# A batch-2 decode block on one core: the last V block moved ahead of half of wo, the attention tail made uniform, and the gated MLP computed as rows

## The chip, the cores and the metric

The kernel runs on one core of one Trainium2 chip. The metric is device time in microseconds (us) of one execution, median of several. "Span" is the time from the first to the last instruction in the one profiled execution; it is about 2 us shorter than the timed figure. TensorE, VectorE and ScalarE are PE, DVE and ACT in the profile's lines, the DMA-issuing engine is SP.

## The reference, cut to what matters

```python
# x: (2, 1, 512) bf16; K and V caches: (2, 32, 8192, 128) bf16; wq: (512, 4096); wo: (4096, 512)
# W_gate, W_up: (512, 1376); W_down: (1376, 512)
q = layernorm(x) @ wq                        # 32 heads of 128
p = softmax(q . K^T * 128**-0.5)             # one query per head, 8192 keys
h = x + (p . V) @ wo
y = layernorm(h)
out = h + (relu(y @ W_gate) * (y @ W_up)) @ W_down
```

K and V are 268 MB; all weights together are 12.6 MB. The heads are worked off in 16 "quads" of four heads (eight per batch row). One quad's K is 8 MB (8 x 2^20 bytes, and so wherever this text says MB of a load), its V another 8 MB.

## The kernel before

VectorE multiplies each K tile by the replicated query and adds along the head dimension; ScalarE exponentiates; TensorE multiplies the weights into V. K tiles rotate through two buffers, V through one. The main loop (cut):

```python
    for n in range(N - 1):                    # N = 16 quads
        scores(n, HALVES if n == 0 else (0, T))
        if n + 2 < N:
            load_k(n + 2)                     # waits until scores(n) has read its buffer
        collect()                             # VectorE: pick the lanes out of a finished V product
        ...                                   # gather, normalise, at chosen n
        weighted_v(n)
        if n + 2 < N:
            load_v(n + 1)                     # waits until weighted_v(n) has read the one V tile
```

After the loop everything that follows attention goes into the K buffer that quad 14 leaves, and the DMA queue gets, in this order: all of wo, the last V in four pieces, gate, up, W_down.

```python
    W = kring.tile([P, RING], bf16, tag="k", name="W")
    ...                                       # wo of quads 0-3, 4-5, 6 in rows of 16, 8, 4 KB
    nc.sync.dma_start(out=wol, in_=A_wo[LQ * G * Dh:, :].rearrange("(h d) n -> d h n", d=P))  # 1 KB rows
    CUTS = (0, T // 2, T * 7 // 8, T * 15 // 16, T)
    load_v(N - 1, CUTS)
    ...                                       # gate, up, W_down
    scores(N - 1)
    ...
    for k in range(NK):                       # 28 wo matmuls: 7 of 8 quads of both batch rows
        g = k % (P // Q) * Q
        nc.tensor.matmul(out=ar_ps[g:g + B], lhsT=oc[:, k, :], rhs=wo_sb[:, k, :], ...)
    ar = opool.tile([P, D], f32, tag="row")
    nc.scalar.activation(out=ar, in_=ar_ps, func=ACT.Copy)
    o15 = ps_o.tile([P, TG * Dh], f32, tag="o")
    v_moving(N - 1, o15, 0, CUTS[1], last=False)          # V15, first half
    for c in range(KC):                                   # rows to columns, f32
        nc.tensor.matmul(out=a_ps[:, c, :], lhsT=columns(ar)[:, c, :], rhs=row_of[:, 0:B], ...)
    ...
    v_moving(N - 1, o15, CUTS[1], CUTS[2], first=False)   # V15, up to 7/8
    o_sum = lanes_of(o15)
    ...                                                   # the last eighth with V stationary
    for h in range(G):                                    # the last quad alone: 16 small matmuls
        project(wol[:, h, :], ol[:, h, :], last=(h == G - 1))
```

So only the last quad's share, 16 bf16 matmuls with wo stationary, stands between V15 and the second layernorm. The MLP keeps its weights stationary: 44 matmuls of 128x128 by 2 columns each for gate and for up, and the results lie as columns, 11 blocks by 2, ready for W_down.

The softmax here doesn't subtract the row's maximum and nothing guards it: scores larger than these inputs give would overflow.

## Time and profile before

| | before |
|---|---|
| time, median | 661.2 us |
| span of the profiled execution | 659.4 us |
| DMA, 281 MB | busy in every part of the span but the end |
| VectorE busy | 609.6 us (92%) |
| TensorE busy | 119.5 us (18%) |

The first lines are from the page of the kernel before: the span, then busy tenths in 40 slices for VectorE and DMA.

```profile
span 659.4 us, 3234 instructions
...
DVE  2899999999999999999999999999999998999952
...
DMA  9999999999999999999999999999999999999996
```

DMA is full from beginning to end. To see how the stream runs I added up the bytes of the trace's DMA packets in order of their end: 8 MB land every 19.35 us, one load behind the other. By this count the bytes up to the end of each of the last loads have landed at these times (us from the span's start): K15 594.98, V14 613.9, all of wo 624.1, V15 643.2, gate 646.7, up 650.0, W_down 655.2. Neighbouring loads overlap, so a load's own last packet can come later than its count (gate 648.15, up 651.50). 8,388,608 bytes in 19.35 us are 433.5 GB/s. The Trainium skill ("DMA: Bandwidth & Descriptors", Where 436 GB/s comes from) gives 435.2 GB/s as the ceiling of the ports into SBUF; the trace agrees to within half a per cent, so rearranging work can gain at most half a per cent in the middle of the kernel.

What is left is the end. The chain of waits of the kernel before, from 560 us on (start, duration, what):

```profile
554.14 41.31 DMA k<-in_A_k_cache_dram
...
595.47 17.24 DVE k L222
...
629.57 2.29 DVE sc L231
...
636.38 3.16 PE ar_ps L452 x28
...
642.02 1.96 PE a_ps L459 x8
...
645.75 0.36 DVE osb L266
...
648.37 0.67 PE a_ps L434 x16
...
650.34 1.71 PE gate_ps L510 x44
...
654.38 1.17 PE y_ps L466 x31
...
655.55 0.52 PE y_ps L466 x12
```

K15 is released at 554.14 and lands 41 us later: the queue is that far ahead, and what VectorE does between two quads is hidden by it. From 595.47 VectorE works 36.4 us on quad 15; from 631.86 a chain of short TensorE and VectorE links follows. It ends at 656.38, just after the stream does at 655.2: compute and DMA end together.

### The profile page before, as it was taken

How to read it: one execution, taken by the hardware profiler on the slowest of the kernel's cores; microseconds unless marked ns; L12 is line 12 of the kernel's file. 1: busy time of each engine (PE TensorE's matmuls, PEld its weight loads, DVE VectorE, ACT ScalarE, POOL GpSimd, SP SyncE). 2: the span in 40 equal slices, each digit the busy share in tenths (PEclk: the TensorE clock that was granted, in tenths of full speed). 3: DMA queues.
4: the chain of work that ended last, by engine and by line, in shares of the span. 5: the costliest groups of instructions: out<-in, count | busy, mean ns of one | idle time of the engine just before them, and what ended most of it. 6: DMA issues, size and time to landing. Idle time of an engine off the chain costs nothing.

```text
span 659.4 us, 3234 instructions
## 1 busy us (share of the span) xinstructions
PE 119.5 (18%) x1341; PEld 58.6 (9%) x1341; DVE 609.6 (92%) x225; ACT 55.8 (8%) x142; POOL 2.5 (0%) x8
## 2 busy tenths in 40 slices
PE   2100302003030210303012130301202030020446
PEld 1000101001010100101001110100001010010225
DVE  2899999999999999999999999999999998999952
ACT  2201001010101001010101001010010101001020
POOL 1000000000000000000000000000000000000000
PEclk9555755757565575756557575555757555575656
DMA  9999999999999999999999999999999999999996
GB/s 382 445 445 445 395 433 446 437 445 418 417 445 437 441 442 398 445 445 426 441 417 433 445 422 441 437 417 441 426 441 441 421 438 426 433 441 433 393 420 259
DMA packets 7314, 281.26 MB, mean 427 GB/s; under 512 B 802, under 2 KB 1412, under 8 KB 2308
## 3 DMA queue, kind: packets, MB, share of 16 engines
q1 hardware_dynamic: 7272, 281.06, 98.9%
q8 instruction: 10, 0.16, 0.1%
q14 instruction: 4, 0.03, 0.0%
q10 hardware_dynamic: 28, 0.01, 0.0%
HBM read 281.06 MB, written 0.00 MB: 426 GB/s over the span
## 4 chain that ended last, share of the span: by engine, by line
DVE 62%; DMA 33%; PE 3%; issue 1%; ACT 0%; DVEq 0%
DMA k<-in_A_k_cache_dram 31%; DVE k L222 29%; DVE k L228 28%; DVE sc L231 4%; DMA wq_sb<-in_A_wq_dram 2%; DVE osb L268 1%; DVE qrep L188 1%; PE qps L175 1%; PE o L257 1%; PE ar_ps L452 0%; ACT qrep L186 0%; PE y_ps L466 0%; PE a_ps L459 0%; PE gate_ps L510 0%; PE up_ps L510 0%
## 5 line engine op out<-in xcount | busy, mean ns | idle before, releaser
L222 DVE TENSOR_TENSOR k<-k,qrep 128x32768 bf16<-128x32768 bf16 (+1 forms) x17 | 275.7, 16217 | 8.9 <-DMA k<-in_A_k_cache_dram 8.8
L228 DVE TENSOR_TENSOR k<-k 128x16384 bf16<-128x16384 bf16 (+3 forms) x68 | 266.8, 3923 | 2.3
L257 PE MATMUL o<-v,pm 128*32 128x512 bf16 x1016 | 88.1, 522 | 395.8 <-DMA v<-in_A_v_cache_dram 395.8
L234 ACT ACTIVATE pm<-sc 32x256 bf16<-32x256 f32 x64 | 47.2, 738 | 563.9 <-DVE sc L231 527.6
L257 PEld LDWEIGHTS <-pm 128*32 128x32 bf16 x1016 | 37.9, 127 | 444.8 <-issue 282.3
L231 DVE TENSOR_REDUCE sc<-k 128x256 f32<-128x2048 bf16 (+1 forms) x17 | 36.7, 2161 | 1.6
L307 PE MATMUL rep<-osb,spread 128*64 128x128 f32 (+1 forms) x16 | 5.9, 474 | 110.5 <-DVE osb L268 110.5
L234 ACT ACTIVATION_READ_ACCUMULATOR pm<-sc 32x1 f32 x64 | 15.0, 234 | 0.0
L307 PEld LDWEIGHTS rep<-osb,spread 128*64 128x64 f32 (+1 forms) x16 | 3.2, 257 | 114.1 <-DVE osb L268 114.1
L188 DVE CAST qrep<-qps 32x512 bf16<-32x512 f32 x8 | 5.5, 692 | 7.2 <-ACT qrep L186 7.1
L266 DVE TENSOR_SCALAR osb<-o,turn_of 128x128 f32<-128x128 f32 x10 | 3.4, 344 | 9.2 <-PE o L257 9.2
L268 DVE SCALAR_TENSOR_TENSOR osb<-o,turn_of,osb 128x128 f32<-128x128 f32 x30 | 10.5, 351 | 1.1
L175 PE MATMUL qps<-wq_sb,xnb 128*64 128x512 bf16 x32 | 6.5, 562 | 7.0 <-DMA wq_sb<-in_A_wq_dram 4.8
L186 ACT ACTIVATE qrep<-qps 32x512 bf16<-32x512 f32 x8 | 4.7, 586 | 8.5 <-PE qps L175 5.2
L152 DVE COPY xc<-x_ps 128x8 f32<-128x8 f32 x1 | 0.2, 167 | 4.9 <-PE x_ps L149 4.9
L510 PEld LDWEIGHTS <-W 128*128 128x128 bf16 (+1 forms) x88 | 3.8, 126 | 0.3 <-issue 0.3
L175 PEld LDWEIGHTS <-xnb 128*64 128x64 bf16 x32 | 2.7, 147 | 10.0 <-issue 5.3
L452 PE MATMUL ar_ps<-W,oc 128*2 128x512 bf16 x28 | 3.2, 626 | 1.8 <-DVE oc L357 1.8
L297 PE MATMUL o_l<-lane_of,osb 128*128 128x4 f32 x2 | 0.6, 364 | 12.8 <-DVE osb L268 12.8
L317 DVE TENSOR_TENSOR rep<-rep,pick 128x128 f32<-128x128 f32 x6 | 1.8, 295 | 1.0 <-PE rep L307 0.9
L330 PE MATMUL zb<-zm,same 128*128 128x4 f32 (+2 forms) x12 | 2.3, 306 | 0.3 <-DVE ol_f L298 0.3
L330 PEld LDWEIGHTS zb<-zm,same 128*128 128x128 f32 x12 | 2.1, 258 | 0.8 <-issue 0.4
(92 smaller groups left out, 44.3 us busy)
## 6 DMA issues: line engine op xcount, KB each, us to landing
k<-in_A_k_cache_dram SPq DMA_DIRECT2D x2, 4096.0 KB
wq_sb<-in_A_wq_dram SPq DMA_DIRECT2D x1, 4096.0 KB, 12.3
v<-in_A_v_cache_dram SPq DMA_DIRECT2D x1, 4096.0 KB, 13.3
v<-in_A_v_cache_dram SPq DMA_DIRECT2D x1, 3072.0 KB, 20.2
W<-in_A_wo_dram SPq DMA_DIRECT2D x1, 2048.0 KB
W<-in_B_W_gate_dram SPq DMA_DIRECT2D x1, 1376.0 KB
W<-in_B_W_up_dram SPq DMA_DIRECT2D x1, 1032.0 KB, 27.4
W<-in_A_wo_dram SPq DMA_DIRECT2D x1, 1024.0 KB, 29.0
```

The source lines that it names most:

```text
L175: nc.tensor.matmul(out=qps[h * B * Q:(h + 1) * B * Q], lhsT=xnb[:, c].rearrange("p b q -> p (b q)"), rhs=wq_v[:, c, g:g + QP, h0 + h, :], ...
L186: nc.scalar.activation(out=dst, in_=src, func=ACT.Copy)
L188: nc.vector.tensor_copy(dst, src)
L222: nc.vector.tensor_tensor(out=kp, in0=kp, in1=_view(qrep[:, b, i, :], 0, [[0, hi - lo], [1, Dh]]), op=ALU.mult)
L228: nc.vector.tensor_tensor(out=kp[:, :, 0:half], in0=kp[:, :, 0:half], in1=kp[:, :, half:width], op=ALU.add)
L231: nc.vector.tensor_reduce(out=sc[:, lo:hi], in_=kp[:, :, 0:8], axis=AXIS.X, op=ALU.add)
L234: nc.scalar.activation(out=p_of[ps, :, :, h], in_=sc[ps, :].rearrange("p (g t) -> p g t", t=TG), func=ACT.Exp, accum_out=(zm[ps, b, i:i + ...
L257: nc.tensor.matmul(out=o[g:g + W2], lhsT=_view(pm, (0 if lane else R) + t // TG * W2, [[1, W2]]), rhs=vt[:, t:t + TG, :].rearrange("p t d ...
L268: nc.vector.scalar_tensor_tensor(out=osb, in0=o[:, t * Dh:(t + 1) * Dh], scalar=turn_of[:, t:t + 1], in1=osb, op0=ALU.mult, op1=ALU.add)
L307: nc.tensor.matmul(out=reps[where][at:at + m, max(k - 1, 0), :], lhsT=spread[n_of].rearrange("k u h m -> k (u h m)"), rhs=osb, start=True, ...
L330: nc.tensor.matmul(out=zb, lhsT=lhsT, rhs=z, start=True, stop=True)
L510: nc.tensor.matmul(out=ps[0:w, fc, :], lhsT=lhsT, rhs=hd[:, c, :], start=(c == 0 and fc == 0), stop=(c == KC - 1), skip_group_check=True)
```

## The change

Its intent: treat all eight quads of a row alike, so that one piece of code serves them (gathers of four quads, no special last quad, fewer masks); have V15 earlier, by loading it into V14's tile half by half ahead of the second half of wo; and compute gate and up as rows, 512 columns at a time in three column tiles of TensorE, then transpose the activations back with four matmuls. The diff, cut to its core ("..." marks cuts):

```diff
-    SIZES = (4, 2, 1)
-    FIRST = (0, 4, 6)
+    NS = 4
...
+    load_wo(0)
+    L = N - 1
+    vts[L] = vts[L - 1]
+    weighted_v(L - 1, 0, T // 2)
+    load_part(vts[L], A_v_cache, L, 0, T // 2)
+    weighted_v(L - 1, T // 2, T)
+    CUTS = (T // 2, T * 7 // 8, T)
+    for lo, hi in zip(CUTS[:-1], CUTS[1:]):
+        load_part(vts[L], A_v_cache, L, lo, hi)
+    for k in range(1, NGR):
+        load_wo(k)
+    scores(L)
+    X = kring.tile([P, RING], bf16, tag="k", name="X")      # gate, up, W_down: K15's buffer
...
+    attention_rows(0, NK - JG)                               # first 16 of 32 wo matmuls
+    for lo, hi in zip(CUTS[:-1], CUTS[1:]):
+        weighted_v(L, lo, hi)
     collect()
+    gather()
+    normalize(B - 1, NGR - 1)
+    attention_rows(NK - JG, NK)                              # the other 16
     ar = opool.tile([P, D], f32, tag="row")
     nc.scalar.activation(out=ar, in_=ar_ps, func=ACT.Copy)
...
-    for h in range(G):
-        project(wol[:, h, :], ol[:, h, :], last=(h == G - 1))
+    for c in range(KC):
+        nc.tensor.matmul(out=h_ps[:, c, :], lhsT=ar.rearrange("p (m c) -> p c m", c=KC)[:, c, :],
+                         rhs=row_of[:, 0:B], start=(c == 0), stop=True, skip_group_check=True)
...
+            for j in range(FT):
+                nc.tensor.matmul(out=ps[j * Q:(j + 1) * Q, :],
+                                 lhsT=hd[:, c].rearrange("p a b -> p (a b)"),
+                                 rhs=wgu[:, g, c, offs[j]:offs[j] + MT], ...)
...
+    for r in range(RD):
+        nc.tensor.matmul(out=act_ps[:, r].rearrange("p j b -> p (j b)"),
+                         lhsT=act[0:RW].rearrange("k (m r) -> k r m", r=RD)[:, r, :], rhs=ident..., ...)
```

## The prediction

> **What bounds it now.** The page gives DMA at 9 tenths in 39 of 40 slices and 281 MB, so the stream sets the pace. Adding up the trace's packets in order, 8 MB land every 19.35 us, without a gap, from the first load on: K15 at 594.98, V14 at 613.9, wo at 624.1, V15 at 643.2, gate 646.7, up 650.0, W_down 655.1. The queue is some 40 us ahead (K15 issued at 554.1, landed at 595), so VectorE's small work between quads is hidden. The chain ends: DMA k to 595.45, VectorE scores(15) 36.4 us to 631.86, then 24.5 us of short TensorE and VectorE links to 656.38, output, span 659.4 (661.2 timed). There compute and DMA finish together: the last y_ps matmul waits for the last W_down rows.
>
> **What moves.**
> 1. Masks, collects (10 to 8), gathers, normalising in the loop: some 3 us less VectorE. Off the path: K15's landing does not move. Worth 0.
> 2. V15's first half waits for half of V14's matmuls (start 614.97, 99 ns each: 618.2), while wo's first half is through at 618.3. With the issue, a DMA gap of 1 to 2 us (estimate). Given back: wo's last quad had 1 KB rows and took 2.15 us for 0.5 MB against 1.2 for 0.5 MB of others. W_down still ends near 655.
> 3. Gate, up and W_down now go into K15's tile, so after 631.86; the queue holds V15 and wo until about 644. Gate about 647.5, up 651: before their use.
> 4. Tail. Before, 28 of 32 wo matmuls and their row-to-column products ran before V15's last part; now half of wo, the whole gather and the columns come after it. From the trace's durations (estimate): Exp ends 634.99; z sums and 32 V matmuls to 638.8; x row and 16 wo matmuls (113 ns each) to 640.9; 32 V matmuls to 642.8; four lane steps 1.5, spread 0.8, gather 0.6, normalise 0.2: 646; 16 wo matmuls 1.8; ScalarE copy 0.6; columns 2.0 (the trace: 8 in 2.03); copy, sum, mean 1.0; hd 0.25: 651.7.
> 5. MLP in: 12 matmuls of 512 columns, three side by side. Four side by side take 427 ns a round at clock 0.5, so four rounds 1.7 us for gate, 1.7 for up, against 1.71 and 1.59 before. No gain. The elementwise steps are 512 wide instead of 22: about 0.65 instead of 0.25 each (the 32x512 cast took 0.69), gate's hidden under up. New: four transposing matmuls and a copy, 0.8. Down 48 matmuls, 1.6. End near 658.5, plus 3 us of output.
>
> So some 2 us slower, unless the clock helps. The Trainium skill ("TensorE: Matmul & The Clock Gate", Part 1) says the clock is released by activity in free-running windows of 3413 ns. This trace agrees: 0.91 to 1.00 from 640 to 647, 0.50 before and after 649. Cold for wo and MLP is what I assume; warm would save about 2.5 us.
>
> **Predicted: 663.2 us, 80% range 660.9 to 665.0.** Faster by over 2%: 0.005; within 2%: 0.985; slower by over 2%: 0.01.
>
> **What would show it.** scores(15) ends within 0.5 us of 631.9; DMA shows a dip at 618 to 620 and ends near 655; last lane steps start near 642.9 (before: 645.75); gate_ps starts near 652 (before: 650.34) and takes about 1.7; y_row near 658.5, waiting for compute, not DMA.
>
> **What would make it wrong.** The gap at 618 longer than 3 us, so that wo's second half or gate becomes the wait; three column tiles not running side by side (gate 5 us); fp32 column products cheaper than 2 us; a warm clock through the MLP, giving equality or a small gain.

## The result

The changed kernel takes 663.33 us (median of 6, 662.55 to 663.95) against 661.25 us (median of 6, 661.01 to 661.45): 2.1 us or 0.3% slower. The ratio is 1.0032, with a 95% interval of 1.0019 to 1.0044. Ratios in this text are the mean time of one kernel's runs over that of the kernel before's runs of the same rounds, so they are not quite the ratios of the medians quoted. Executions over 1.5% slower than the fastest of the same kernel are left out of the means. Every variant below gave a correct result.

The page of the changed kernel:

```profile
span 661.5 us, 2931 instructions
...
DVE  2899999999999999999899998999899998999932
...
DMA  9999999999999999999999999999999999999896
```

Both kernels start on quad 15 at the same time. This is VectorE's timeline around the start of quad 15, first of the kernel before, then of the changed kernel; the bracket says how long VectorE waited and for what.

```profile
595.47 17.23 DVE L222 TENSOR_TENSOR k<-k,qrep 128x32768 bf16<-128x32768 bf16 x1 [1.24 <-DMA k<-in_A_k_cache_dram]
```

```profile
595.48 17.22 DVE L214 TENSOR_TENSOR k<-k,qrep 128x32768 bf16<-128x32768 bf16 x1 [0.92 <-DMA k<-in_A_k_cache_dram]
```

595.47 and 595.48: all that the change saved on VectorE in the loop (604.7 us busy against 609.6) moved nothing, as VectorE waits for the stream in both. The whole 2.1 us arise after this point. The chain of waits of the changed kernel from 560 us on:

```profile
614.88 5.27 PE o L244 x63
...
620.63 25.26 DMA W<-in_A_wo_dram
...
645.94 1.91 PE ar_ps L390 x16
...
648.52 2.04 PE h_ps L405 x8
...
650.58 0.18 DVE hc L408
...
652.23 1.70 PE gate_ps L438 x12
...
656.11 0.70 DVE act L456
...
657.42 0.87 PE y_ps L428 x48
...
658.38 0.29 DVE y_row L471
```

The chain now runs through DMA until 645.94: the second sixteen wo matmuls wait for the second half of wo. The timeline shows the same wait in its bracket, while V15's matmuls ended early:

```profile
640.09 1.90 PE L244 MATMUL o<-v,pm 128*32 128x512 bf16 x32
...
644.74 0.24 DVE L314 TENSOR_SCALAR oc<-ou,zi 128x16 bf16<-128x16 f32 x1
645.04 0.08 PEld L390 LDWEIGHTS <-oc 128*2 128x2 bf16 x1 [1.24 <-DVE oc L314]
645.94 1.88 PE L390 MATMUL ar_ps<-W,oc 128*2 128x512 bf16 x16 [1.89 <-DMA W<-in_A_wo_dram]
```

The bracket's 1.89 us is all the idle time before these matmuls. Their own input (oc, the normalised quad) was ready at 645.04, where TensorE loaded its first weights, so 0.9 us of it are the wait for wo. wo's last packet ended at 645.43; here, as in the last waits of e3 and e5 below, the first matmul that needs a load starts 0.5 us after the load's last packet. The late landing has its origin at 618 us, in these one-microsecond stretches (length, busy time and count of PE, PE weight loads, DVE, ACT and POOL, then granted clock, DMA share, GB/s), first before, then after:

```profile
617.00:618.00 1.00, 1.00 (x16) 0.45 (x12) 1.00 (x1) 0.00 (x0) 0.00 (x0) 0.50 0.88 369
618.00:619.00 1.00, 1.00 (x16) 0.45 (x12) 1.00 (x1) 0.00 (x0) 0.00 (x0) 0.50 1.02 418
```

```profile
617.00:618.00 1.00, 1.00 (x16) 0.50 (x12) 1.00 (x1) 0.00 (x0) 0.00 (x0) 0.50 0.65 262
618.00:619.00 1.00, 1.00 (x24) 0.46 (x16) 1.00 (x1) 0.00 (x0) 0.00 (x0) 0.91 0.31 131
```

The dip is the 262 and 131 GB/s. V15's first half is issued at 618.44, when TensorE is through half of V14, and its first packet starts at 619.40; by then the DMA engines that had finished wo's first half had nothing to do: of the usual 16 packets in flight, 8 were left at 618.2 and one at 619.2. By the count of bytes, the stream took 29.35 us from the end of V14 to the end of V15 and wo before, and 30.69 us after.

### The profile page after: what moved, and what is told of

Same layout as the page of the kernel before. It is cut to its first block, busy times and chain, and to the rows that moved or that the text cites. A ratio compares the mean times of both kernels' runs of the same rounds, so it can differ in the third digit from the quotient of the medians.

```text
span 661.5 us, 2931 instructions
## 1 busy us (share of the span) xinstructions
PE 117.5 (18%) x1211; PEld 51.3 (8%) x1211; DVE 604.7 (91%) x188; ACT 55.8 (8%) x142; POOL 4.3 (1%) x8
## 4 chain that ended last, share of the span: by engine, by line
DMA 75%; PE 15%; another core or an unknown queue 8%; DVE 1%; ACT 0%; issue 0%; SPq 0%; DVEq 0%
DMA v<-in_A_v_cache_dram 69%; PE o L244 13%; DMA W<-in_A_wo_dram 4%; DMA wq_sb<-in_A_wq_dram 2%; PE qps L168 0%; DVE qrep L181 0%; PE h_ps L405 0%; PE ar_ps L390 0%; ACT qrep L179 0%; PE gate_ps L438 0%; PE up_ps L438 0%; PE y_ps L428 0%; DVE act L456 0%; ACT ar L401 0%
## 5 line engine op out<-in xcount | busy, mean ns | idle before, releaser
L244 PE MATMUL o<-v,pm 128*32 128x512 bf16 x1024 | 93.6, 545 | 410.4 <-DMA v<-in_A_v_cache_dram 410.4
L244 PEld LDWEIGHTS <-pm 128*32 128x32 bf16 x1024 | 39.3, 130 | 463.2 <-issue 289.4
L284 PE MATMUL rep<-osb,spread 128*64 128x128 f32 x16 | 5.2, 423 | 97.4 <-DVE osb L255 97.4
L284 PEld LDWEIGHTS rep<-osb,spread 128*64 128x64 f32 x16 | 2.2, 198 | 101.3 <-DVE osb L255 61.9
L255 DVE SCALAR_TENSOR_TENSOR osb<-o,turn_of,osb 128x128 f32<-128x128 f32 x24 | 8.4, 351 | 0.8
L365 POOL MEMSET X<- 40x2048 bf16 x1 | 1.8, 1797 | 628.9 <-DVE sc L223 628.9
L405 PE MATMUL h_ps<-row_of,ar 128*128 128x2 f32 x8 | 2.0, 375 | 0.7 <-ACT ar L401 0.7
```

The lines of the kernel that those rows point to most:

```text
L244: nc.tensor.matmul(out=o[g:g + W2], lhsT=_view(pm, (0 if lane else R) + t // TG * W2, [[1, W2]]), rhs=vt[:, t:t + TG, :].rearrange("p t d ...
L255: nc.vector.scalar_tensor_tensor(out=osb, in0=o[:, t * Dh:(t + 1) * Dh], scalar=turn_of[:, t:t + 1], in1=osb, op0=ALU.mult, op1=ALU.add)
L284: nc.tensor.matmul(out=state["rep"][u * m:(u + 1) * m, :], lhsT=spread.rearrange("k u h m -> k (u h m)"), rhs=osb, start=True, stop=True, ...
```

## The experiments

Twelve kernels, each timed in five rounds against the kernel before on the same chip (three calls of four, the kernel before at 661.33, 661.38 and 661.28 us). The changed kernel itself stands at 663.33 us, ratio 1.0032. The intervals of the ratios are about plus or minus 0.0013, so variants that differ by half a microsecond are told apart by their profiles more than by their times.

| run | edit | us | ratio to before |
|---|---|---|---|
| e1_wo_piece | changed; 0.5 MB of wo's second half ahead of V15 | 662.48 | 1.0018 |
| e2_old_mlp | changed; MLP of before | 662.94 | 1.0022 |
| e3_ar_bf16 | changed; attention rows in bf16 | 662.79 | 1.0024 |
| e4_wo_ahead | changed; all of wo ahead of V15 | 665.23 | 1.0062 |
| e5_wd_order | changed; W_down's short block first | 664.08 | 1.0044 |
| e6_ar_wd | e3 and e5 | 664.24 | 1.0043 |
| e7_all | e6, and 1 MB of wo ahead of V15 | 662.89 | 1.0029 |
| e8_before_ar_wd | before; bf16 rows, W_down's short blocks first | 660.16 | 0.9982 |
| e9_before_align | before; K and V tiles at a multiple of 512 bytes | 659.76 | 0.9977 |
| e10_after_align | changed; K and V tiles at a multiple of 512 bytes | 662.04 | 1.0008 |
| e11_ar_spread | e3, W_down's short block cut to use 16 engines | 662.75 | 1.0020 |
| e12_best | changed; bf16 rows, 1 MB of wo ahead, cut block, aligned tiles | 660.60 | 0.9992 |

### e1_wo_piece: work for the queue while V15 waits

```diff
     load_wo(0)
+    load_wo1(0, 4)                 # 4 of 16 rows per partition of wo's second half
     ...                            # V15 as in the changed kernel
-    for k in range(1, NGR):
-        load_wo(k)
+    load_wo1(4, JG)
```

> The changed kernel with a quarter of the second half of wo (0.5 MB) loaded ahead of the last V, so that the DMA queue has work while V15's first half waits for V14's matmuls; all else alike. Theory A (the tail's serial chain is the cost, and 0.9 us of it is a wait for wo's second half made by the DMA gap at 618 to 621): the gap closes, V15 still lands near 640, wo's last rows land about 1 us earlier, the second sixteen wo matmuls start right after the normalised quad (no DMA wait before them; before the edit 0.9 us) and the time falls by 0.5 to 1.0 us, to about 662.5. Theory B (the MLP's new form is the cost, the DMA order is harmless): no change, 663.3.

Measured 662.48 us. The dip is gone (the same one-microsecond stretches of this run):

```profile
617.00:618.00 1.00, 1.00 (x16) 0.41 (x12) 1.00 (x1) 0.00 (x0) 0.00 (x0) 0.50 0.94 393
618.00:619.00 1.00, 1.00 (x16) 0.51 (x12) 1.00 (x1) 0.00 (x0) 0.00 (x0) 0.50 0.85 340
```

and in the chain of waits the wo matmuls follow the normalised quad directly:

```profile
645.74 0.25 DVE oc L314
...
646.03 1.06 PE ar_ps L397 x16
```

Two things moved, though. V15's matmuls ended 1.0 us later in this execution, because the full clock came at 640.68 instead of 638.66; and the second sixteen wo matmuls fell into the full clock and took 1.06 us instead of 1.91. So the wait is shown to come from the gap, but the 0.9 us of the median cannot all be put down to it: wo's last packet ended only 0.6 us earlier (644.85 against 645.43).

### e2_old_mlp: the MLP alone undone

```diff
-    hd = opool.tile([P, KC, NR, B], bf16, tag="hd")        # replicated, for the row form
+    hd = misc.tile([P, KC, B], bf16)
...                                  # gate, up, act, W_down's loads and y_rows as in the kernel before
```

> The changed kernel with the MLP of the kernel before (gate, up and W_down with the weights stationary or in ten blocks, no row form, no transposes); attention tail and DMA order as changed. Theory A: the MLP accounts for 0.8 us of the 2.1 us (from the end of the column products to the end of the output row 8.1 us against 7.3), so the time falls to about 662.5 and the chain before gate_ps does not move. Theory B: the whole loss goes, 661.3.

Measured 662.94 us. TensorE's timeline of this run:

```profile
651.60 1.74 PE L432 MATMUL gate_ps<-hd,X 128*128 128x2 bf16 x44
...
653.63 1.71 PE L432 MATMUL up_ps<-hd,X 128*128 128x2 bf16 x44
655.67 1.34 PE L416 MATMUL y_ps<-X,act 128*2 128x128 bf16 x44 [0.33 <-DVE act L451]
```

From the evacuated columns (hc, 650.01) to the output row (657.13) it takes 7.1 us, against 7.8 us in the changed kernel (650.58 to 658.38) and 7.0 in the kernel before (649.08 to 656.09). So the row form costs 0.7 to 0.8 us in these executions: little of it in its matmuls (gate 1.90 us in 12 matmuls against 1.71 in 44), most in the two elementwise steps over 512 columns (0.75 and 0.68 us, the first of them hidden) and the transposing matmuls with their copy. It is not the whole loss, and the rival theory falls. The 0.8 us expected in the time did not show: the median fell by only 0.4 us, and the intervals of the two ratios overlap. In the profiled execution, 662.20 us, K15 also landed 0.4 us earlier than in the changed kernel, which is not the MLP's doing. Nor was the clock the same: the changed kernel's down matmuls ran at full clock (0.84 us), those of this run at half (1.34 us). The size of the MLP's share is thus read from the profiles and not settled by the times.

### e3_ar_bf16: the rows-to-columns products in one pass

```diff
-    ar = opool.tile([P, D], f32, tag="row")
+    ar = opool.tile([P, D], bf16, tag="row")
+    row_b = consts.tile([P, Q], bf16)
+    nc.vector.tensor_copy(row_b, row_of)
...                                  # row_b instead of row_of in the two products with ar
```

> The changed kernel with the attention rows ar evacuated as bf16 instead of f32, so that the products that turn rows to columns are 4 bf16 matmuls instead of 8 fp32 passes (and likewise the 4 y_rows). Theory A: these products lie on the chain with 2.03 us and fall to about 0.5; the four y_rows fall too (0.65 to 0.25); W_down's landing (656.6, used at 657.4) then becomes the wait, so the time falls by 1.0 to 1.6 us, to about 662.0. Theory B: they are hidden, no change.

Measured 662.79 us: 0.5 us, less than expected. TensorE's timeline:

```profile
647.84 0.29 PE L407 MATMUL h_ps<-row_b,ar 128*128 128x2 bf16 x4 [0.70 <-ACT ar L403]
...
649.61 1.90 PE L440 MATMUL gate_ps<-X,hd 128*32 128x512 bf16 x12 [0.15 <-DVE hd L414]
...
655.15 0.60 PE L430 MATMUL y_ps<-X,act_t 128*2 128x128 bf16 x16 [0.27 <-DVE act_t L467]
656.03 0.60 PE L430 MATMUL y_ps<-X,act_t 128*2 128x128 bf16 x16 [0.28 <-DMA X<-in_B_W_down_dram]
656.91 0.62 PE L430 MATMUL y_ps<-X,act_t 128*2 128x128 bf16 x16 [0.29 <-DMA X<-in_B_W_down_dram]
```

The products fell from 2.03 to 0.29 us and gate starts 2.4 us earlier (649.61 against 652.02). But the last matmuls then wait for W_down, twice, as the brackets say: its last packets end at 656.75. Most of the gain on the chain is lost to the stream's end. The changed kernel is bound by compute, but its stream ends only about a microsecond before its last data are needed. (Of the 2.4 us, 1.7 are the products; most of the rest is the full clock, which in this execution covered the second sixteen wo matmuls as well.)

### e4_wo_ahead: the old order of wo and V15

```diff
-    load_wo(0)
+    for k in range(NGR):
+        load_wo(k)
     L = N - 1
...
-    for k in range(1, NGR):
-        load_wo(k)
```

> The changed kernel with all of wo ahead of the last V, as the kernel before has it. Theory A: no DMA gap, but V15 lands at about 643.5 instead of 639.9, its second half of matmuls ends near 645 instead of 642, and the serial chain behind it moves with it: slower by 1.5 to 3 us, about 665.3. If instead the order of wo and V is what cost the 2.1 us, this run is faster, about 661.5.

Measured 665.23 us, 1.9 us slower than the changed kernel, as expected. Its chain of waits:

```profile
645.03 0.36 DVE osb L253
...
648.01 1.06 PE ar_ps L388 x16
```

The lanes start at 645.03 instead of 642.05 and every later link of the attention tail moves with them. The new order of loads is right for the new tail; what costs is that the new tail has so much behind V15.

### e5_wd_order and e6_ar_wd: an attempt to end the stream earlier, which failed

```diff
-    for j in range(FT):                        # W_down's three blocks: 128, 128 and 88 partitions
+    ORDER = [FT - 1] + list(range(FT - 1))     # the short one first, in loads and in matmuls
+    for j in ORDER:
```

> The changed kernel with W_down's small last block (0.34 MB on 88 partitions, in two pieces) loaded and used first of the three, so that the stream ends with a full 0.5 MB block; nothing else. Theory A (compute is the last to finish in the changed kernel, the stream is 0.8 us ahead of it): the stream ends 0.5 to 1 us earlier than 656.6 and the time stays, 663.3. Rival (the stream's later end, 656.6 against 655.1 before, is what makes the changed kernel slower): the time falls by 0.7 to 1.4 us, to about 662.3.

> As the run above, with the attention rows in bf16 as well. Theory A with the stream as the second limit: bf16 rows alone gave 0.5 us of the 1.6 us that its chain lost, because W_down landed at 656.7; with W_down earlier the rest comes: 1.0 to 1.6 us below the changed kernel, about 662.0. If W_down's end was not the limit there: no gain over bf16 rows alone, 662.8.

Both were slower: 664.08 and 664.24 us. The stream did not end earlier but 1.5 us later (last W_down packet at 658.12 against 656.67), and the matmuls, in order, had a whole block left to do behind it. This is e5's TensorE timeline:

```profile
657.26 0.62 PE L429 MATMUL y_ps<-X,act_t 128*2 128x128 bf16 x32 [0.28 <-DVE act_t L466]
658.62 0.45 PE L429 MATMUL y_ps<-X,act_t 128*2 128x128 bf16 x16 [0.75 <-DMA X<-in_B_W_down_dram]
```

So neither theory was tested as planned; what the runs do show is that the end of the stream binds when it comes 1.5 us later: e5's last matmuls wait for it until 658.62, and the time rises by 0.7 us. Up to the transposed activations e5 was no slower than the changed kernel (down matmuls start at 657.26 against 657.42).

The packet records show one irregularity: the block on 88 partitions is carried by 11 engines. At 654.5 us of the changed kernel, 12 packets are in flight instead of 16, 11 of them of this block. The Trainium skill ("DMA: Bandwidth & Descriptors", Why a DMA increments its semaphore by 16 and not by 1) says that a transfer takes the largest number of engines up to 16 that divides the outermost dimension of both its source and its destination; for 88 that is 11, and the trace agrees.

### e7_all and e8_before_ar_wd

> Both edits of the run above and half of wo's second half (1 MB) ahead of the last V. Theory A: the costs found add up; no DMA wait before the second sixteen wo matmuls, bf16 rows, W_down's end near 655: about 661.2, equal to the kernel before (661.3) and not clearly below it, because the stream still ends near 655.

> The kernel before with the same two edits where they apply: attention rows in bf16, W_down's short last blocks loaded and used first. Theory A (before, stream and compute end together, the last matmuls wait for W_down's last rows at 655.1): each alone would give next to nothing, both together 0.5 to 1.2 us: about 660.4, the fastest version. If the kernel before is bound by neither: 661.3.

e7 missed: 662.89 us instead of 661.2. It carries e5's order of W_down with it, and its last matmuls wait for W_down until 657.2; from up to W_down the stream took 6.7 us, as against 5.4 in the changed kernel.

e8 met its number, 660.16 us, but not for the reason given. Its VectorE starts on quad 15 at 594.26, 1.2 us earlier than the kernel before, and from there to the end of the span it takes 64.1 us, against 64.0 before (658.32 and 659.43 less the starts). The edits to the tail gained nothing in the end. They did shorten the chain: counted from the start of quad 15, the columns (hc) come 2.6 us earlier (645.30 against 649.08; 1.7 us of it are the products, 0.30 us instead of 2.03). But all of this is spent waiting for gate, up and W_down (0.85, 0.70, 0.47 and 0.86 us), as e8's TensorE timeline shows:

```profile
647.15 1.75 PE L511 MATMUL gate_ps<-hd,W 128*128 128x2 bf16 x44 [0.85 <-DMA W<-in_B_W_gate_dram]
...
654.43 0.59 PE L467 MATMUL y_ps<-W,act 128*2 128x128 bf16 x16 [0.86 <-DMA W<-in_B_W_down_dram]
```

So in e8 the stream's end is the limit, and a shorter chain alone gains nothing. The gain lies in the 590 us in front of the tail, which the edits do not touch. There, 8 MB landed every 19.32 us instead of 19.35. The one thing that had changed for these loads was where they land (the addresses are those of the built programs): the 64 bytes per partition of the new row_b had moved the K and V tiles from byte 29,632 to 29,696 of their partitions, a multiple of 1024.

### e9_before_align and e10_after_align: the place of the tiles

```diff
+    misc2 = ctx.enter_context(tc.tile_pool(name="misc2", bufs=1))   # behind the rings
-    oc = misc.tile([P, NK, B], bf16)
+    oc = misc2.tile([P, NK, B], bf16)
...                                  # ou, gate, act, hd alike: K tiles at byte 29,184 = 57 x 512
```

> The kernel before with five small tiles (oc, ou, gate, act, hd) allocated behind the rings instead of ahead of them, so that the K and V tiles start at a multiple of 512 bytes in each partition (before: 64 bytes past a multiple of 128; in the kernel before with bf16 rows, which was 1.2 us faster, the added 64-byte tile had moved them onto a multiple of 1024). No instruction changes. Theory C (that run's gain came from the place of the tiles and not from its edits: its 8 MB loads landed every 19.32 us instead of 19.35, 30 times): 8 MB per 19.32 us, K15 lands about 1 us earlier, 660.2. Rival (its edits to the tail made the gain): no change, 661.3.

```diff
+    pad = consts.tile([P, 16], bf16)            # 32 bytes: K tiles from byte 24,032 to 24,064 = 47 x 512
+    nc.gpsimd.memset(pad, 0.0)
```

> The changed kernel with 32 unused bytes per partition, so that its K and V tiles start at a multiple of 512 bytes (as changed: 32 bytes past a multiple of 64, 19.36 us per 8 MB). Theory C: about 1.2 us less, 662.1, the tail as it was. Rival: 663.3. In either case the place of the tiles does not explain the change's 2.1 us, as K15 lands at 595.0 in both kernels.

Measured 659.76 us for the kernel before with moved tiles (0.9977, interval 0.9965 to 0.9990) and 662.04 us for the changed kernel with the pad. VectorE's timeline at the start of quad 15, first of e9, then of e10:

```profile
594.04 17.23 DVE L223 TENSOR_TENSOR k<-k,qrep 128x32768 bf16<-128x32768 bf16 x1 [0.81 <-DMA k<-in_A_k_cache_dram]
```

```profile
594.41 17.22 DVE L216 TENSOR_TENSOR k<-k,qrep 128x32768 bf16<-128x32768 bf16 x1 [0.88 <-DMA k<-in_A_k_cache_dram]
```

1.4 and 1.1 us earlier than in the kernels that they were made of; some 1.0 and 1.2 us are what 0.034 and 0.040 us on each of 30 loads make (an estimate), and the rest is within the small pauses that differ between executions. In the four runs with tiles at a multiple of 512 bytes (e8, e9, e10, e12) 8 MB land every 19.32 us; where the tiles start at a multiple of 32 bytes only (changed kernel, e3, e11 and others), every 19.36; at an odd multiple of 64 (before) or of 128 (e2), every 19.35. Theory C holds, in both kernels. The Trainium skill ("DMA: Bandwidth & Descriptors", How a descriptor splits into AXI transactions) describes 256-byte transactions that must start at multiples of 256, for reads; e2's 24,192, a multiple of 128 but not of 256, at 19.35 us fits a boundary at 256 or 512 on the written side, but no run here tells 256 from 512. As the tiles of both original kernels are unaligned (19.353 and 19.359 us, at most 0.2 us over 30 loads), and K15 lands within 0.05 us in both profiled executions, this has next to no part in the change's 2.1 us. The times say the same: with aligned tiles in both, the changed kernel is still 2.3 us slower (e10 662.04, e9 659.76).

### e11_ar_spread and e12_best

```diff
-        for r0, r1 in ((0, RD),) if j < FT - 1 else ((0, RD - 1), (RD - 1, RD)):
-            nc.sync.dma_start(out=wd_sb[p0:, j, r0:r1], in_=rows[:, r0:r1])
+        pe = (p0 + 15) // 16 * 16               # 88 partitions as 8 and 80
+        for q0, q1, r0, r1 in (((0, P, 0, RD),) if j < FT - 1 else
+                               ((p0, pe, 0, RD), (pe, P, 0, RD - 1), (pe, P, RD - 1, RD))):
+            nc.sync.dma_start(out=wd_sb[q0:q1, j, r0:r1], in_=rows[q0 - p0:q1 - p0, r0:r1])
```

> The changed kernel with bf16 rows (662.8 alone, where W_down's end at 656.7 was the limit) and W_down's last block, 352 rows on 88 partitions, cut into 8 and 80 partitions, so that it goes over 16 engines instead of 11. If the 11 engines make the stream's end late: W_down ends at about 656.0 and the time falls to about 662.2. If the last block is slow only because it is last and small: no change, 662.8.

> The changed kernel with all that helped: half of wo's second half ahead of the last V, bf16 rows, the spread last block, and K and V tiles at a multiple of 512 bytes. The gains add (0.5 to 0.9, 0.5, 0.5, 1.2 us): about 660.3, below the kernel before by 1 us and equal to the kernel before with aligned tiles.

e11: 662.75 us, no gain over e3's 662.79. By the count of bytes it took 5.3 us from up to W_down, in e3 5.9, in the changed kernel 5.4 and in e12, with the same cut, 6.0: the 11 engines are real, but nothing shows that they cost time here. The last 0.34 MB take 2.4 to 3.3 us in the runs that load this block last (2.7 before, in another shape). The packet records show part of the reason. Of the usual 16 packets in flight only one or two are left some 0.6 us before the end, before, after and in e3, e11 and e12 alike, which suggests that one or two engines work off their rest alone. Why these have more left than the others stays open. e12: 660.60 us, 0.9992 with an interval of 0.9978 to 1.0005, which is level with the kernel before and not clearly below it; it gains 2.7 us on the changed kernel. It was expected to equal the kernel before with aligned tiles (e9) and stays 0.8 us above it. Its chain of waits is nearly all stream:

```profile
640.30 14.19 DMA X<-in_B_W_down_dram
...
654.62 0.42 PE y_ps L441 x16
...
655.14 0.29 DVE y_row L484
```

The fastest version of all is the kernel before with its tiles moved, 659.76 us, without one instruction changed.

## Why the prediction was right

The time, 663.3 us, is close to the predicted 663.2. The mechanism is the predicted one: the stream sets the pace up to quad 15, and a longer chain behind V15 and a row form without gain make the tail longer. That it fits to 0.1 us is luck, as errors in the steps cancelled. Step by step:

1. Less VectorE work in the loop is worth nothing: right. VectorE lost 4.9 us of busy time, more than the 3 us estimated, and quad 15 starts at 595.48 against 595.47.
2. A DMA gap of 1 to 2 us at 618: right; the stretch from V14 to the end of V15 and wo took 1.3 us longer. That it would be given back, with W_down still ending near 655: wrong. The missing 1 KB rows of wo were expected to return about 1 us, but the whole stretch before was only 0.3 us above its bytes' worth (12 MB at 19.35 us per 8 MB are 29.03 us, it took 29.35), so there was little to return. W_down ended at 656.7 (655.2 before).
3. Gate and up land before their use: right, by 3.3 and 2.1 us (last packets at 648.75 and 652.14, first matmuls at 652.02 and 654.27). wo's second half I had put at "about 644" and thought of as a wait only if the gap were longer than 3 us; its last packet ended at 645.43, the matmuls could use it from 645.94, and they were ready at 645.04. This is the term that the sum lacked: 0.9 us (e1 removes the wait).
4. The tail: gate_ps predicted near 652, measured 652.02. Two errors cancelled. V15's matmuls ended 0.75 us earlier than predicted (lanes at 642.05; 642.8 predicted), because the full clock came at 638.66 and also covered the first sixteen wo matmuls (1.03 us instead of 1.7). The wait for wo took this back. The column products on the chain with 2.0 us: right (2.03; e3 takes 1.7 us of it off the chain).
5. The MLP: gate 1.90 us and up 1.74 where 1.7 each were predicted, with the variance matmuls (0.4 us) between them, which the sum left out; the elementwise steps 0.75 and 0.68 (0.65); transposes and copy 0.56 (0.8). The down matmuls took 0.84 us, not 1.6, because the clock was full again from 655.72, which made up for the longer gate and up. Three column tiles do run side by side: a round of three begins every 0.43 us at half clock. Net cost against before 0.8 us from hc to the output row; e2's profile gives 0.7.

Adding up from the traces: from the last Exp to hc 15.6 us after (634.98 to 650.58) against 14.1 before (634.98 to 649.08), so 1.5 us for the attention tail; 0.8 us for the MLP; together 2.3 us, of which the output at the end takes back about 0.3. The time is shown to lie in these two stretches; e1 and e3 show two parts of the first (the wait for wo, the f32 products). That the rest of it is the removed shortcut for the last quad (16 stationary matmuls in 0.67 us instead of gather, sixteen row matmuls, a copy and the products) is read from the timelines and was not undone by itself. Part of the 1.5 us also hangs on where the full clock fell: the second sixteen wo matmuls took 1.88 us at half clock in the changed kernel's profile, 1.03 at full clock in e3.

The text called 640 to 647 "0.91 to 1.00" of the clock; the window boundaries were in another place in each execution (full clock from 640.95 before, 638.66 after, 640.68 in e1). The Trainium skill ("TensorE: Matmul & The Clock Gate", Part 1) calls the windows free-running, and the traces agree. It probably explains much of the changed kernel's wider spread (1.4 us against 0.4), since its tail has more full-width matmuls; no run tests this.

## What to carry to other kernels

When a stream of loads fills the whole kernel, read how far ahead the queue is before pricing anything in the loop, and then price the end twice: the chain of compute behind the last big load, and the stream's own end; a gain on one is capped by the other. A load that waits for compute in its own buffer needs other work queued in front of it for that time, or its gap moves everything that comes behind. And when a variant gains, check in which stretch: here a "tail" edit won 1.2 us in the loads before the tail, by shifting a tile by 64 bytes.

## What the Trainium skill lacked or had wrong

- "DMA: Bandwidth & Descriptors" (Constraints and How a descriptor splits into AXI transactions) speaks of alignment for transposes and for reads; it has no figure for where a plain load's destination starts in SBUF. Here 8 MB took 19.32 us at multiples of 512 bytes and 19.35 to 19.36 us otherwise: 0.2% of the stream, about 1.0 to 1.2 us over 30 loads (an estimate from these figures), beside measured gains of 1.2 to 1.5 us in e8, e9 and e10.
- The same page gives 435.2 GB/s as the ceiling and, in its 16 MB measurement, 425 GB/s; the aligned stream here held 8,388,608 bytes per 19.32 us, 434.2 GB/s, in 27 of e9's 29 intervals between loads.
- The same page's rule for the number of engines was confirmed (88 partitions: 11), but it doesn't say what a short transfer at the end of a stream costs behind other loads: 0.34 MB took 2.4 to 3.3 us as the last load, cut for 11 engines or for 16, against 0.8 us at the stream's rate (an estimate from 19.35 us per 8 MB), and some 0.6 us before the end only one or two packets were in flight.
- "TensorE: Matmul & The Clock Gate" was right where it was used; nothing to correct.
